# Two-bank AV tiles, half a mask on ScalarE, a new order of the first loads, and an earlier load for batch 1, in a pooled-attention and MLP kernel

## The chip, the cores and the metric

The kernel runs on one core of one Trainium2 chip. The time is device microseconds (us) of one execution; of the 60 runs of the kernel before that stand beside v_noact, 57 lie within 0.3% of their median of 300.84. Engines: PE (TensorE), PEld (its weight loads), DVE (VectorE), ACT (ScalarE), POOL (GpSimd) and SP (SyncE, which here only issues loads, stores and transposes by DMA). Every run comes with a state, fast or slow; a run is called slow when it is over 1.5% above the fastest of its kernel. Ratios in this text are the mean time of one kernel's fast runs over the mean time of the other's fast runs of the same rounds, so they are not quite the ratio of the medians that are quoted beside them. The span of a profile is some 1.7 us shorter than the time.

## The reference

```python
# q, k, v: (8 batches, 8 heads, 576 tokens, 64)
k_p = k.reshape(B, H, S // 8, 8, D).mean(axis=3)      # keys and values are pooled by 8: 72 of each
v_p = v.reshape(B, H, S // 8, 8, D).mean(axis=3)
scores = np.matmul(q, k_p.transpose(0, 1, 3, 2)) / np.sqrt(D)
attn = np.exp(scores - max) / sum                     # softmax
x = np.matmul(attn, v_p)                              # "AV"; then laid out as (4608 tokens, 512)
h = x @ w_in                                          # 512 -> 2048
return (h - np.tanh(h)) @ w_out                       # 2048 -> 512
```

The 72 pooled keys of a head are handled as 64 in four tiles (two heads to a tile) and the 8 that are left over, which are called the leftover keys.

## The kernel before

The MLP of one batch is one long run of matmuls on PE. Attention of the next batch is woven into it. Batch 0 has nothing to be woven into, so its attention, the *front*, is on the path; batch 1's loads are on their way meanwhile. Some words: an *hT* matmul belongs to x @ w_in and an *o_ps* matmul to the product with w_out; the AV matmuls write x; to *turn* x is to transpose it on PE, after which ACT copies (*evacuates*) it from PSUM; `warm_pe(n)` issues n filler matmuls whose result nobody uses; the *tail* of q is its last 64 tokens of a batch. The parts that matter:

```python
    # loads of batch 0: SP and ACT issue them in this order
    load_main(k_pairs, k_raw[0], 0, 0, 1); load_q0(0, 2)
    load_main(k_pairs, k_raw[0], 0, 1, 2); load_q0(2, 4)
    load_main(k_pairs, k_raw[0], 0, 2, 4)
    load_q0(4, 8)                                     # second half of q, from ACT
    load_dense(k_pairs, k_raw[0], 0, nc.scalar)       # leftover keys
    load_dense(v_pairs, v_raw[1], 0, nc.scalar)
    ...
    after(load_k(1), w1_dmas[1])                      # k of batch 1 once w1's second chunk is in
    load_q(1, False)                                  # q of batch 1 without its tail, from SP
    load_main(v_pairs, v_raw[1], 1, 0, NM)
    ...
    nc.scalar.dma_start(out=t0[:QT, :, R, :], ...)    # tail of q, batch 0, from ACT
    ...
    v_main(VB[0], vs, nc.vector, 0, 2)                # mask of v, two instructions on DVE
    v_main(VB[0], vs, nc.vector, 2, 4)
    load_left(v_pairs, v_raw[1], 1, nc.scalar)        # four small loads of batch 1, issued by ACT
    load_q_tail(1, q_raws[1], nc.scalar)              # tail of q of batch 1, issued by ACT
    ...
    av_half(0, 0, 0, xs[0], ps_all)                   # AV: eight half blocks, a PSUM bank each
    av_half(0, 1, 0, xs[1], ps_all)
    av_half(0, 2, 0, xs[2], ps_all)
    x_pe_transpose(0, 0, xs[0], (0, 2))               # transposed on PE, evacuated by ACT into xT
    ...
```

An engine issues its loads in the order of its own instruction stream.

The softmax here doesn't subtract the row's maximum and nothing guards it: scores larger than these inputs give would overflow.

Of the kernel before, what the change touches and what calls it, by code (L numbers as in the profile page):

```python
# [8 lines left out]
FP32 = mybir.dt.float32  # L9
BF16 = mybir.dt.bfloat16  # L10
ACT = mybir.ActivationFunctionType
ALU = mybir.AluOpType
# [25 lines left out]
def kernel(  # L38
# [19 lines left out]
    ps_h = ctx.enter_context(tc.tile_pool(name="ps_h", bufs=3, space=PSUM))  # L58
    ps_o = ctx.enter_context(tc.tile_pool(name="ps_o", bufs=2, space=PSUM))
    ps_a = ctx.enter_context(tc.tile_pool(name="ps_a", bufs=3, space=PSUM))  # L60
# [19 lines left out]
    q_bf = const.tile([128, R + 1, H, D], BF16, name="q_bf")  # L80
    warm = const.tile([128, 1], FP32, name="warm")
# [156 lines left out]

    def v_left(vb, vs, eng):
        eng.tensor_tensor(  # L240
            out=vb[:, 2 * NM :, 0:D],
            in0=vs.to_broadcast([128, NM, D]),
            in1=mask[:, 2 * NM :, :].to_broadcast([128, NM, D]),
            op=ALU.mult,
        )
# [92 lines left out]
    def av_half(b, blk, half, x_sb, alloc):  # L338
        E = E_tiles[b]
        vb = VB[b % 2]  # L340
        c0 = blk * 128 if blk < 4 else S - 128
        ps = alloc([128, 4, D1], FP32, "x_ps")
        for n in range(3):
# [14 lines left out]
        rden = work.tile([128, 4, 1], FP32, name="rden", tag="rden", bufs=4)  # L358
        nc.vector.reciprocal(out=rden[:, :, :], in_=ps[:, :, D:D1])  # L359
        nc.vector.tensor_tensor(  # L360
            out=x_sb[:, half, :, :],
            in0=ps[:, :, 0:D],
            in1=rden[:, :, :].to_broadcast([128, 4, D]),
            op=ALU.mult,
        )
# [56 lines left out]
    def mlp_h_mms(g, i, f0, f1, pool=None):  # L422
        tok0 = g * TG
        if f0 == 0:
            p, tag = pool or (ps_h, "hT_ps")
            h_tiles[i] = p.tile([128, TG], FP32, name="hT_ps", tag=tag)
# [96 lines left out]
    warm_ps = ps_o.tile([128, 512], FP32, name="warm_ps", tag="o_ps")  # L523
# [21 lines left out]
    load_q0(2, 4)  # L545
    load_main(k_pairs, k_raw[0], 0, 2, 4)
    load_q0(4, 8)
    load_dense(k_pairs, k_raw[0], 0, nc.scalar)
    load_dense(v_pairs, v_raw[1], 0, nc.scalar)
# [3 lines left out]
    nc.scalar.activation(out=warm[:, :], in_=warm[:, :], func=ACT.Exp)  # L553
    nc.vector.memset(KB[0][:, :], 0.0)
# [37 lines left out]
    after(load_k(1), w1_dmas[1])  # L592
# [49 lines left out]
    q_turn(nc.scalar.copy, 6, 8)  # L642
    pool_k(0, nc.vector, 2, 4)
    warm_pe(6)
    k_turn(2, 4)
    pool_k(0, nc.vector, NM, NT)
    warm_pe(2)
    q_pe_transpose(0, (2, 3), "act")
    warm_pe(2)
    scores_wide(0, (2, 3))  # L650
    k_turn_left()
    warm_pe(2)
    v_ps = v_pe_pool(NM, NT, spread)
    scores_wide(0, (NM,))
    v_left(VB[0], v_ps[:, 0, :, :], nc.vector)
    vs = v_pe_pool(0, NM, ident)
    v_main(VB[0], vs, nc.vector, 0, 2)
    v_main(VB[0], vs, nc.vector, 2, 4)
    load_left(v_pairs, v_raw[1], 1, nc.scalar)
    load_q_tail(1, q_raws[1], nc.scalar)  # L660
    xs = [new_x() for _ in range(4)]
    gts = []
    ps_o2 = lambda sh, dt, name: ps_o.tile(sh, dt, name=name, tag="o_ps")
    ps_h2 = lambda sh, dt, name: ps_h.tile(sh, dt, name=name, tag="hT_ps")
    warm_pe(2)
    av_half(0, 0, 0, xs[0], ps_all)
    av_half(0, 1, 0, xs[1], ps_all)
    av_half(0, 2, 0, xs[2], ps_all)
    x_pe_transpose(0, 0, xs[0], (0, 2))
    av_half(0, 3, 0, xs[3], ps_all)  # L670
    warm_pe(1)
    x_pe_transpose(0, 1, xs[1], (0, 2))
    ps_any = ps_b1
    av_half(0, 0, 1, xs[0], ps_h2)
    warm_pe(1)
    x_pe_transpose(0, 2, xs[2], (0, 2))
    av_half(0, 1, 1, xs[1], ps_b1)
    warm_pe(1)
    x_pe_transpose(0, 3, xs[3], (0, 2))
    av_half(0, 2, 1, xs[2], ps_o2)  # L680
    mlp_h_mms(0, 0, 0, 2)
    x_pe_transpose(0, 0, xs[0], (2, 4))
    av_half(0, 3, 1, xs[3], ps_b1)
    mlp_h_mms(0, 1, 0, 2)
    x_pe_transpose(0, 1, xs[1], (2, 4))
    mlp_h_mms(0, 2, 0, 2)
    x_pe_transpose(0, 2, xs[2], (2, 4))
# [117 lines left out]
```

## Time and profile before

| kernel before | |
|---|---|
| time, median of 3 runs | 301.34 us (301.06 to 301.42) |
| span of the profile | 299.1 us |
| PE busy | 291.5 us (97%) |
| first AV matmul of batch 0 | 14.61 us |
| PE without a break from | 20.41 us |
| waits of PE after that | near 32.5 and 37 us, 0.5 and 0.7 us (from matmul start to matmul start) |

The lines behind this are in the prediction below. In an order of time stand start, length, engine, line, operation; ACTq is ACT's sequencer, which issues the loads.

```profile
16.28 0.62 ACTq L127 DMA_DIRECT2D q_raw<-in_q_dram  x1
16.95 0.92 ACT L397 CAST xT<-xT_ps 128x256 bf16<-128x256 f32 x3 [3.19 <-PE x_ps L346]
```

L127 is the issue of the q tail of batch 1. It happens at 16.28 us because the q tail of batch 0 landed at 16.26, and the two share a semaphore (the trace, which keeps the semaphore of each issue, has both on number 100). The evacuations of the transposed x stand behind it. The second is DVE's pooling of v of batch 1:

```profile
42.32 0.82 DVE L219 TENSOR_TENSOR v_raw<-v_raw 128x640 f32<-128x640 f32 x1
...
44.31 0.42 DVE L240 TENSOR_TENSOR VB<-v_raw,mask 128x256 bf16<-128x256 f32 x1
```

### The profile page before, as it was taken

Reading aid. Unit: us, or ns where it says so; the run is one execution under the profiler, and the core shown is the slowest. Engines: PE = TensorE matmul, PEld = TensorE weight load, DVE = VectorE, ACT = ScalarE, POOL = GpSimd, SP = SyncE. Lnnn points to the kernel's source line nnn. Section 1 sums busy time; section 2 is a strip of 40 time slices with the busy share of each in tenths; the row PEclk is TensorE's granted clock in tenths of the full one; section 3 lists DMA queues with packets and bytes.
Section 4 is the critical chain, followed back from the end, with each engine's and each line's share of the span. In section 5 each row is a group of like instructions: output and inputs, shape, how many; then the busy total and the mean of one; then the engine's idle time right before and its main releaser. Section 6 shows DMA issues by size and latency. Waiting matters only on the chain.

```text
span 299.1 us, 4694 instructions
## 1 busy us (share of the span) xinstructions
PE 291.5 (97%) x1671; PEld 142.5 (48%) x1671; DVE 159.1 (53%) x343; ACT 149.4 (50%) x283; POOL 115.5 (39%) x110
## 2 busy tenths in 40 slices
PE   7989999999999999999999999999999999999994
PEld 3454455544544454445444554455445544444443
DVE  5658665673547444753476247716680758108600
ACT  4647583666146633654265516650665166126511
POOL 8500904871496109922971089307940000000000
PEclk9999999999999999999999999999999999999999
DMA  7999999849854998699648974897431430111032
GB/s 251 226 211 278 311 227 310 263 87 328 234 113 99 271 297 134 117 302 245 107 88 235 300 167 94 242 294 159 97 66 35 95 92 0 37 70 36 0 72 70
DMA packets 66183, 49.79 MB, mean 166 GB/s; under 512 B 39920, under 2 KB 52976, under 8 KB 66160
## 3 DMA queue, kind: packets, MB, share of 16 engines
q1 hardware_dynamic: 58832, 42.94, 56.0%
q0 software_dynamic: 4752, 4.72, 9.4%
q10 hardware_dynamic: 2576, 1.84, 2.3%
q8 instruction: 13, 0.21, 0.3%
q14 instruction: 10, 0.08, 0.1%
HBM read 36.70 MB, written 9.44 MB: 154 GB/s over the span
## 4 chain that ended last, share of the span: by engine, by line
PE 85%; DMA 9%; POOL 4%; issue 0%; SPq 0%; ACT 0%; DVE 0%; POOLq 0%
PE o_ps L456 40%; PE hT_ps L428 37%; DMA w1b<-in_moe_w_in_dram 4%; PE x_ps L346 4%; DMA k_raw<-in_k_dram 4%; PE s_ps L298 3%; POOL k_raw L198 1%; DMA out_dram<-o_sb 1%; POOL k_raw L203 1%; POOL kd L206 1%; POOL w2b L510 0%; PE xT_ps L390 0%; POOL v_raw L576 0%; PE qT_ps L171 0%; POOL w1b L503 0%
## 5 line engine op out<-in xcount | busy, mean ns | idle before, releaser
L456 PE MATMUL o_ps<-w2b,gT 128*128 128x512 bf16 x560 | 134.4, 380 | 0.0
L441 DVE TENSOR_TENSOR gT<-hT_ps,t_sb 128x512 bf16<-128x512 f32 x144 | 98.9, 691 | 57.7 <-ACT t_sb L439 57.6
L428 PE MATMUL hT_ps<-xT,w1b 128*128 128x512 bf16 x576 | 126.9, 379 | 0.3 <-ACT xT L397 0.3
L439 ACT ACTIVATE t_sb<-hT_ps 128x512 f32<-128x512 f32 x144 | 85.6, 597 | 38.3 <-PE hT_ps L428 37.5
L428 PEld LDWEIGHTS <-w1b 128*128 128x128 bf16 x576 | 55.9, 98 | 66.5 <-issue 0.4
L456 PEld LDWEIGHTS <-gT 128*128 128x128 bf16 x560 | 52.5, 98 | 52.0 <-issue 1.4
L465 ACT COPY o_sb<-o_ps 128x512 f32<-128x512 f32 x33 | 19.3, 585 | 75.2 <-PE o_ps L456 75.2
L359 DVE RECIPROCAL rden<-x_ps 128x4 f32<-128x4 f32 x80 | 14.2, 177 | 52.5 <-PE x_ps L346 52.0
L360 DVE TENSOR_TENSOR x_sb<-x_ps,rden 128x256 bf16<-128x256 f32 x80 | 34.0, 425 | 3.5 <-DMA xT<-x_sb 0.6
L148 POOL CAST q_bf<-q_raw 128x2048 bf16<-128x2048 f32 x6 | 11.3, 1888 | 59.9 <-issue 34.8
L198 POOL TENSOR_TENSOR k_raw<-k_raw 128x1280 f32<-128x1280 f32 x7 | 20.2, 2886 | 27.4 <-DMA k_raw<-in_k_dram 16.6
L317 ACT ACTIVATE E<-s_ps 128x288 bf16<-128x288 f32 x60 | 21.4, 410 | 13.2 <-PE s_ps L298 13.0
L346 PE MATMUL x_ps<-VB,E 128*128 128x130 bf16 x240 | 20.8, 221 | 0.4 <-ACT xT L397 0.3
L346 PEld LDWEIGHTS <-E 128*128 128x128 bf16 x240 | 16.9, 98 | 8.8 <-DVE VB L230 0.6
L216 POOL TENSOR_TENSOR v_raw<-v_raw 128x1280 f32<-128x1280 f32 x6 | 17.4, 2898 | 0.0
L298 PE MATMUL s_ps<-qT,KB 128*128 128x288 bf16 (+5 forms) x128 | 17.0, 290 | 0.2
L298 PEld LDWEIGHTS <-KB 128*128 128x128 bf16 (+1 forms) x128 | 7.0, 96 | 10.2 <-issue 3.5
L527 PE MATMUL warm_ps<-xT 128*128 128x512 bf16 x29 | 10.2, 465 | 1.3 <-DVE xT L539 1.3
L206 POOL TENSOR_TENSOR kd<-k_raw 128x640 bf16<-128x640 f32 x7 | 10.8, 1540 | 0.5
L203 POOL TENSOR_TENSOR k_raw<-k_raw 128x640 f32<-128x640 f32 x7 | 10.8, 1541 | 0.5
L397 ACT CAST xT<-xT_ps 128x256 bf16<-128x256 f32 (+1 forms) x14 | 5.8, 436 | 8.5 <-PE xT_ps L390 5.1
L219 POOL TENSOR_TENSOR v_raw<-v_raw 128x640 f32<-128x640 f32 x6 | 9.3, 1544 | 0.5
(73 smaller groups left out, 100.7 us busy)
## 6 DMA issues: line engine op xcount, KB each, us to landing
k_raw<-in_k_dram SPq DMA_DIRECT2D x7, 1024.0 KB, 5.9
q_raw<-in_q_dram SPq DMA_DIRECT2D x7, 1024.0 KB, 10.2
v_raw<-in_v_dram SPq DMA_DIRECT2D x7, 1024.0 KB, 9.3
out_dram<-o_sb SPq DMA_DIRECT2D x38, 128.0 KB, 2.4
out_dram<-o_sb SPq DMA_DIRECT2D x16, 256.0 KB, 3.7
w1b<-in_moe_w_in_dram POOLq DMA_DIRECT2D x4, 512.0 KB, 14.2
w2b<-in_moe_w_out_dram POOLq DMA_DIRECT2D x4, 512.0 KB, 16.9
k_raw<-in_k_dram SPq DMA_DIRECT2D x7, 128.0 KB, 5.8
```

The lines of the kernel that those rows point to most:

```text
L198: first = eng.tensor_tensor(out=r[:, :, 0:4, :], in0=r[:, :, 0:4, :], in1=r[:, :, 4:8, :], op=ALU.add)
L216: eng.tensor_tensor(out=r[:, :, 0:4, :], in0=r[:, :, 0:4, :], in1=r[:, :, 4:8, :], op=ALU.add)
L298: nc.tensor.matmul(dst[p : p + w], lhsT=KB[b % 2][:, o : o + w], rhs=qTs[b][:, m, c0:c1], start=True, stop=True,)
L317: nc.scalar.activation(out=E[:, t, half * hs : (half + 1) * hs], in_=ps[:, :], func=ACT.Exp, scale=SCALE)
L346: nc.tensor.matmul(ps[:, 2 * n : 2 * n + 2, :].rearrange("p h d -> p (h d)") if n < 2 else ps.rearrange("p (a s) d -> p a s d", s=2)[:, :, ...
L359: nc.vector.reciprocal(out=rden[:, :, :], in_=ps[:, :, D:D1])
L360: nc.vector.tensor_tensor(out=x_sb[:, half, :, :], in0=ps[:, :, 0:D], in1=rden[:, :, :].to_broadcast([128, 4, D]), op=ALU.mult,)
L428: nc.tensor.matmul(h_tiles[i][:, :], lhsT=w1b[:, fb, i * 128 : (i + 1) * 128], rhs=xT[:, fb, tok0 : tok0 + TG], start=(fb == 0), stop=(fb ...
L439: nc.scalar.activation(out=t_sb[:, :], in_=h_ps[:, :], func=ACT.Tanh)
L441: nc.vector.tensor_sub(out=gT[:, :], in0=h_ps[:, :], in1=t_sb[:, :])
L456: nc.tensor.matmul(o_ps[:, :], lhsT=gts[i][:, tb * 128 : (tb + 1) * 128], rhs=w2b[:, i, :], start=(i == 0), stop=(i == NHID - 1),)
L465: (nc.vector.tensor_copy if g == 0 and tb % 2 else nc.scalar.copy)(out=o_sb[:, :], in_=o_ps[:, :])
```

## The change

The intent is a shorter front and a filled hole at 37 us. (1) AV of batch 0 works on two blocks at once in tiles of two PSUM banks: four reciprocals and four multiplies on DVE in place of eight each, and larger evacuations of the transposed x. Half of v's mask goes to ACT. (2) The leftover keys are loaded and scored ahead of the second half of k, and the second half of q is issued later. (3) k of batch 1 is released by w1's first chunk. (4) One PSUM tile whose banks are dealt out by hand, which (1) needs. Cut to its core:

```diff
-    ps_h = ctx.enter_context(tc.tile_pool(name="ps_h", bufs=3, space=PSUM))   # and ps_o, ps_a
+    PS = psum.tile([128, 8, 512], FP32, name="PS")
+    ps_h, ps_o, ps_a = Banks(0, 1, 2), Banks(3, 4), Banks(5, 6, 7)            # (shortened)
...
+    def v_main_act(vb, vs, t0, t1):
+        for h in range(2):
+            nc.scalar.activation(
+                out=vb[:, 2 * t0 + h : 2 * t1 : 2, 0:D], in_=vs[:, t0:t1, 0, :],
+                func=ACT.Copy, scale=mask[:, h, :],
+            )
...
+    load_dense(k_pairs, k_raw[0], 0)
     load_main(k_pairs, k_raw[0], 0, 2, 4)
-    load_q0(4, 8)
-    load_dense(k_pairs, k_raw[0], 0, nc.scalar)
-    load_dense(v_pairs, v_raw[1], 0, nc.scalar)
+    load_dense(v_pairs, v_raw[1], 0)
     nc.scalar.activation(out=warm[:, :], in_=warm[:, :], func=ACT.Exp)
+    load_q0(4, 8)
...
-    after(load_k(1), w1_dmas[1])
+    after(load_k(1), w1_dmas[0])
...
+    pool_k(0, nc.vector, NM, NT)
     pool_k(0, nc.vector, 2, 4)
...
-    scores_wide(0, (2, 3))
-    k_turn_left()
+    scores_wide(0, (2, 3, NM))
...
     v_main(VB[0], vs, nc.vector, 0, 2)
-    v_main(VB[0], vs, nc.vector, 2, 4)
+    v_main_act(VB[0], vs, 2, 4)
     load_left(v_pairs, v_raw[1], 1, nc.scalar)
     load_q_tail(1, q_raws[1], nc.scalar)
...
-    av_half(0, 0, 0, xs[0], ps_all)          # eight of these, with their transposes
+    av_pair(0, 0, 0)                         # four of these
+    av_pair(1, 0, 2)
+    av_pair(0, 1, 5)
+    x0_turn((0, 1), 0, 7, nc.scalar.copy)
+    av_pair(1, 1, 0)
+    x0_turn((2, 3), 0, 2, nc.scalar.copy)
+    x0_turn((0, 1), 1, 7, nc.scalar.copy)
...
```

More of the change, by code (lines that the diff above doesn't have):

```diff
@@ L57, with bank, __init__, tile @@
     opool = ctx.enter_context(tc.tile_pool(name="opool", bufs=4))
-    ps_h = ctx.enter_context(tc.tile_pool(name="ps_h", bufs=3, space=PSUM))
-    ps_o = ctx.enter_context(tc.tile_pool(name="ps_o", bufs=2, space=PSUM))
-    ps_a = ctx.enter_context(tc.tile_pool(name="ps_a", bufs=3, space=PSUM))
+    psum = ctx.enter_context(tc.tile_pool(name="psum", bufs=1, space=PSUM))
+    PS = psum.tile([128, 8, 512], FP32, name="PS")
+    def bank(i, shape):
+        n = 1
+        for d in shape[1:]:
+            n *= d
+        v = PS[:, i, 0:n]
+        if len(shape) == 3:
+            return v.rearrange("p (a b) -> p a b", a=shape[1])
+        if len(shape) == 4:
+            return v.rearrange("p (a b c) -> p a b c", a=shape[1], b=shape[2])
+        return v
+    class Banks:
+        def __init__(self, *ids):
+            self.ids, self.n = ids, 0
+        def tile(self, shape, dtype=None, name=None, tag=None):
+            self.n += 1
+            return bank(self.ids[(self.n - 1) % len(self.ids)], shape)
+    ps_h = Banks(0, 1, 2)
+    ps_o = Banks(3, 4)
+    ps_a = Banks(5, 6, 7)
     ctx.enter_context(tc.manual_schedule())
@@ L80 @@
     q_bf = const.tile([128, R + 1, H, D], BF16, name="q_bf")
+    x0 = const.tile([128, 4, 2, 4, D], BF16, name="x0")
     warm = const.tile([128, 1], FP32, name="warm")
@@ L237, in v_main @@
         )
+    def v_main_act(vb, vs, t0, t1):
+        for h in range(2):
+            nc.scalar.activation(
+                out=vb[:, 2 * t0 + h : 2 * t1 : 2, 0:D],
+                in_=vs[:, t0:t1, 0, :],
+                func=ACT.Copy,
+                scale=mask[:, h, :],
+            )
     def v_left(vb, vs, eng):
@@ L338, in av_half, with av_mms @@
     def av_half(b, blk, half, x_sb, alloc):
+        ps = alloc([128, 4, D1], FP32, "x_ps")
+        av_mms(b, blk, half, ps)
+        rden = work.tile([128, 4, 1], FP32, name="rden", tag="rden", bufs=4)
+        nc.vector.reciprocal(out=rden[:, :, :], in_=ps[:, :, D:D1])
+        nc.vector.tensor_tensor(
+            out=x_sb[:, half, :, :],
+            in0=ps[:, :, 0:D],
+            in1=rden[:, :, :].to_broadcast([128, 4, D]),
+            op=ALU.mult,
+        )
+    def av_mms(b, blk, half, ps):
         E = E_tiles[b]
@@ L341, in av_half @@
         c0 = blk * 128 if blk < 4 else S - 128
-        ps = alloc([128, 4, D1], FP32, "x_ps")
         for n in range(3):
@@ L357, in av_half @@
             )
-        rden = work.tile([128, 4, 1], FP32, name="rden", tag="rden", bufs=4)
-        nc.vector.reciprocal(out=rden[:, :, :], in_=ps[:, :, D:D1])
-        nc.vector.tensor_tensor(
-            out=x_sb[:, half, :, :],
-            in0=ps[:, :, 0:D],
-            in1=rden[:, :, :].to_broadcast([128, 4, D]),
-            op=ALU.mult,
-        )
     def new_x():
@@ L424, in mlp_h_mms @@
         if f0 == 0:
-            p, tag = pool or (ps_h, "hT_ps")
-            h_tiles[i] = p.tile([128, TG], FP32, name="hT_ps", tag=tag)
+            h_tiles[i] = ps_h.tile([128, TG]) if pool is None else pool
         for fb in range(f0, f1):
@@ L521, in after @@
             )
-    warm_ps = ps_o.tile([128, 512], FP32, name="warm_ps", tag="o_ps")
+    warm_ps = bank(4, [128, 512])
     def warm_pe(n, cols=512):
@@ L642 @@
     q_turn(nc.scalar.copy, 6, 8)
+    pool_k(0, nc.vector, NM, NT)
     pool_k(0, nc.vector, 2, 4)
-    warm_pe(6)
+    warm_pe(3)
+    k_turn_left()
+    warm_pe(5)
     k_turn(2, 4)
-    pool_k(0, nc.vector, NM, NT)
-    warm_pe(2)
     q_pe_transpose(0, (2, 3), "act")
     warm_pe(2)
-    scores_wide(0, (2, 3))
-    k_turn_left()
+    scores_wide(0, (2, 3, NM))
+    v_ps = v_pe_pool(NM, NT, spread)
+    v_left(VB[0], v_ps[:, 0, :, :], nc.vector)
     warm_pe(2)
-    v_ps = v_pe_pool(NM, NT, spread)
@@ L654 @@
-    scores_wide(0, (NM,))
-    v_left(VB[0], v_ps[:, 0, :, :], nc.vector)
     vs = v_pe_pool(0, NM, ident)
     v_main(VB[0], vs, nc.vector, 0, 2)
-    v_main(VB[0], vs, nc.vector, 2, 4)
+    v_main_act(VB[0], vs, 2, 4)
     load_left(v_pairs, v_raw[1], 1, nc.scalar)
     load_q_tail(1, q_raws[1], nc.scalar)
-    xs = [new_x() for _ in range(4)]
     gts = []
-    ps_o2 = lambda sh, dt, name: ps_o.tile(sh, dt, name=name, tag="o_ps")
-    ps_h2 = lambda sh, dt, name: ps_h.tile(sh, dt, name=name, tag="hT_ps")
@@ L665 @@
-    warm_pe(2)
-    av_half(0, 0, 0, xs[0], ps_all)
-    av_half(0, 1, 0, xs[1], ps_all)
-    av_half(0, 2, 0, xs[2], ps_all)
-    x_pe_transpose(0, 0, xs[0], (0, 2))
-    av_half(0, 3, 0, xs[3], ps_all)
-    warm_pe(1)
-    x_pe_transpose(0, 1, xs[1], (0, 2))
-    ps_any = ps_b1
-    av_half(0, 0, 1, xs[0], ps_h2)
-    warm_pe(1)
-    x_pe_transpose(0, 2, xs[2], (0, 2))
-    av_half(0, 1, 1, xs[1], ps_b1)
-    warm_pe(1)
-    x_pe_transpose(0, 3, xs[3], (0, 2))
-    av_half(0, 2, 1, xs[2], ps_o2)
@@ L681, with av_pair @@
-    mlp_h_mms(0, 0, 0, 2)
-    x_pe_transpose(0, 0, xs[0], (2, 4))
-    av_half(0, 3, 1, xs[3], ps_b1)
-    mlp_h_mms(0, 1, 0, 2)
-    x_pe_transpose(0, 1, xs[1], (2, 4))
-    mlp_h_mms(0, 2, 0, 2)
-    x_pe_transpose(0, 2, xs[2], (2, 4))
-    x_pe_transpose(0, 3, xs[3], (2, 4))
-    mlp_h_mms(0, 3, 0, 2, (ps_o, "o_ps"))
-    mlp_h_mms(0, 4, 0, 2, (ps_o, "o_ps"))
+    def av_pair(p, half, b0):
+        ps = PS[:, b0 : b0 + 2, 0 : 4 * D1].rearrange("p k (h d) -> p k h d", d=D1)
+        for k in range(2):
+            av_mms(0, 2 * p + k, half, ps[:, k, :, :])
+        rden = work.tile([128, 2, 4, 1], FP32, name="rden2", tag="rden2")
+        nc.vector.reciprocal(out=rden[:, :, :, :], in_=ps[:, :, :, D:D1])
+        nc.vector.tensor_tensor(
+            out=x0[:, 2 * p : 2 * p + 2, half, :, :],
+            in0=ps[:, :, :, 0:D],
+            in1=rden[:, :, :, :].to_broadcast([128, 2, 4, D]),
+            op=ALU.mult,
+        )
@@ new lines, in x0_turn @@
+    def x0_turn(blks, half, b0, eng):
+        n = len(blks)
+        ps = bank(b0, [128, 2, n, 128])
+        for i, blk in enumerate(blks):
+            for f in range(2):
+                nc.tensor.matmul(
+                    ps[:, f, i, :],
+                    lhsT=x0[:, blk, half, 2 * f : 2 * f + 2, :].rearrange("p h d -> p (h d)"),
+                    rhs=ident[:, :],
+                    start=True,
+                    stop=True,
+                )
+        c = blks[0] * 128
+        eng(
+            out=xT[:, 2 * half : 2 * half + 2, c : c + n * 128],
+            in_=ps.rearrange("p f i c -> p f (i c)"),
+        )
@@ new lines, in h_open @@
+    def h_open(i, b0):
+        mlp_h_mms(0, i, 0, 2, bank(b0, [128, TG]))
+    warm_pe(2)
+    av_pair(0, 0, 0)
+    av_pair(1, 0, 2)
+    av_pair(0, 1, 5)
+    warm_pe(2)
+    x0_turn((0, 1), 0, 7, nc.scalar.copy)
+    av_pair(1, 1, 0)
+    warm_pe(2)
+    x0_turn((2, 3), 0, 2, nc.scalar.copy)
+    warm_pe(2)
+    x0_turn((0, 1), 1, 7, nc.scalar.copy)
+    h_open(3, 3)
+    h_open(4, 4)
+    x0_turn((2,), 1, 5, nc.scalar.copy)
+    x0_turn((3,), 1, 6, nc.vector.tensor_copy)
+    h_open(2, 2)
@@ L691 @@
+    h_open(0, 0)
+    h_open(1, 1)
+    ps_any = ps_b1
+    ps_h.n = ps_o.n = 0
     nc.scalar.copy(out=q_bf[:QT, R, :, :], in_=t0[:QT, :, R, :])
```

## The prediction

> **What bounds the kernel now.** I read the page's busy table first, then busy time by stage, then each engine's order of time in the first 40 us, and last the chain that ended last. From the page, and from the view by stretches (start:end, length, then busy us of PE, PEld, DVE, ACT, POOL, granted clock, DMA share, GB/s):
>
> ```profile
> PE 291.5 (97%) x1671; PEld 142.5 (48%) x1671; DVE 159.1 (53%) x343; ACT 149.4 (50%) x283; POOL 115.5 (39%) x110
> ...
> 14.60:20.40 5.80, 4.82 (x49) 3.16 (x50) 4.59 (x17) 2.04 (x6) 0.00 (x0) 1.00 1.24 215
> 20.40:32.00 11.60, 11.60 (x72) 5.60 (x68) 8.43 (x15) 8.78 (x17) 1.79 (x1) 1.00 1.16 259
> 32.00:36.90 4.90, 4.58 (x25) 2.05 (x24) 3.24 (x7) 2.54 (x6) 4.81 (x5) 1.00 1.11 332
> 36.90:40.00 3.10, 2.58 (x22) 1.43 (x21) 0.98 (x3) 2.82 (x5) 0.86 (x1) 1.00 1.19 260
> ```
>
> PE is the bound: from 20.4 us on it is full except for two holes near 32.5 and 37 us. The chain's long pieces are 64 hT matmuls in 13.81 us, so 0.216 us each[...]; nothing after 40 us can give anything, because the change leaves the later PE work alone. So the change can gain only (a) in how soon PE gets into its uninterrupted stream of MLP matmuls, and (b) in those holes. The order of time on PE shows both (start, length, count, idle before and who ended it):
>
> ```profile
> 14.61 0.69 PE L346 MATMUL x_ps<-VB,E 128*128 128x130 bf16 x9
> ...
> 18.49 0.59 PE L428 MATMUL hT_ps<-xT,w1b 128*128 128x512 bf16 x2 [0.28 <-ACT xT L397]
> ...
> 20.41 5.78 PE L428 MATMUL hT_ps<-xT,w1b 128*128 128x512 bf16 x26
> ...
> 32.75 0.23 PE L390 MATMUL xT_ps<-ident,x_sb 128*128 128x64 bf16 x2 [0.32 <-DVE x_sb L360]
> ...
> 37.82 0.45 PE L259 MATMUL kT_ps<-ident,kd 128*128 128x128 bf16 x5 [0.52 <-POOL kd L206]
> ```
>
> AV of batch 0 starts at A = 14.61. Six hT matmuls are done before 20.41; from there PE isn't interrupted, so the tenth is issued out at 20.41 + 4 x 0.216 = 21.27, that is A + 6.66. Ten is the count to compare: after ten (five tiles, first half) the changed kernel also runs free. What sets 6.66 is DVE, which takes a half block every 0.55 us, eight times:
>
> ```profile
> 15.00 0.18 DVE L359 RECIPROCAL rden<-x_ps 128x4 f32<-128x4 f32 x1
> 15.22 0.42 DVE L360 TENSOR_TENSOR x_sb<-x_ps,rden 128x256 bf16<-128x256 f32 x1
> 15.56 0.17 DVE L359 RECIPROCAL rden<-x_ps 128x4 f32<-128x4 f32 x1
> ...
> 19.63 0.43 DVE L360 TENSOR_TENSOR x_sb<-x_ps,rden 128x256 bf16<-128x256 f32 x1
> ```
>
> What fixes A is the chain before it: q heads 4 to 7 land at 8.96 (issued 1.84; ACT's cast starts when they do), casts, transposes, scores, then v's pooling on PE (1.05 us) and v's mask on DVE. And the hole at 37 us is the end of a chain of loads (start, length, what):
>
> ```profile
> 8.98 1.14 ACT L610 CAST q_bf<-q_raw 128x512 bf16<-128x512 f32 x2 [0.18 <-DMA q_raw<-in_q_dram]
> ```
> ```profile
> 5.86 12.86 DMA w1b<-in_moe_w_in_dram
> 19.21 10.84 DMA k_raw<-in_k_dram
> 30.21 2.90 POOL k_raw L198
> ...
> 36.23 1.55 POOL kd L206
> ```
>
> Batch 1's k isn't issued until the second chunk of w1 has landed (18.72), lands by 30.05, is pooled on GpSimd until 37.77, and PE waits for it. Counted from matmul start to matmul start the hole is 0.68 us (four o_ps matmuls begin at 36.28, so PE could take the next at 37.14).
>
> [...] 128x256 takes 0.425 us and 128x512 (gT) 0.692, so 1.04 ns an element and 0.158 us fixed. [...] ACT's and DVE's halves of v's mask read one bank. [...] from 5 to 7 us SP's ring (2048-byte packets) moved 0.50 MB and ACT's (1024-byte) 0.26 MB.
>
> **The change part by part.**
>
> 1. *Pairs in AV.* DVE: a pair needs one reciprocal (about 0.18) and one 128x512 multiply, 0.692. Spacing is now 0.548 = 0.217 (reciprocal to multiply) + 0.424 - 0.09 overlap; for a pair 0.217 + 0.692 - 0.09 = 0.82. Four pairs 3.3 us in place of eight halves 4.4. Evacuations of the transposed x fall from eight of 128x256 (0.37 each) to three of 128x512 (0.585) plus one small each on ACT and DVE. The PE work (24 AV matmuls at 0.059, 16 transposes at 0.056) is the same. Walking through from A: first pair's six matmuls end at A+0.51; DVE has x of it at A+0.55+0.91 = A+1.46, the others at 2.28, 3.09, 3.91. PE: three pairs to 1.05, two fillers, transposes of blocks 0-1 at 1.52, fourth pair to 2.09, fillers to 2.52, transposes of 2-3 to 2.74 (end 2.91). ACT evacuates the first by 2.53 and the second from 2.94 to 3.54. Third transposes at 3.18 (x at 3.09). Tile 3's hT opens at 3.59, when ACT is done; tile 4 at 4.02; last four transposes 4.45 to 4.67; the other three tiles to 5.97. The second halves then need x evacuated by 5.3: no wait. So A + 5.97 in place of A + 6.66: 0.69 gained.
>
> 2. *Leftover keys first, q later.* The leftover k goes to SP's queue ahead of the second k half, and heads 4 to 7 of q are issued after the table load, near 3.3 in place of 1.84. DVE's 1.1 us of leftover pooling moves into its wait before 7.86, and the leftover scores follow the others directly. Against it: 0.25 MB (leftover k and v) now stands ahead of q's second half[...]. At 0.34 MB/us (2 MB land between about 2.5 and 8.96) with half the rate after 8 us I put q's landing at 9.6 to 10.4, middle 9.9, in place of 8.96. Then: casts to 11.07, transposes of the last heads to 11.3, ACT's qT to 12.14, scores 11.76 to 12.64, leftover v to 12.88, two fillers (0.43, new there) to 13.31, v's pooling to 14.18 (end 14.35), DVE's mask 0.43 and A = 14.87. ACT's half of the mask[...] comes after DVE's on the same bank[...] and is first needed by the third pair at 15.6: just hidden. So part 2 costs 0.26 where the serial order had hoped to gain; if q lands at 9.0 it gains 0.15.
>
> 3. *Batch 1 sooner.* k waits for w1's first chunk (15.43) rather than its second: 3.3 us sooner. GpSimd then ends near 34.5 and PE's need is near 36.7, so the whole 0.68 us goes. The price is traffic: k competes with w1's third and fourth chunks (22.06 and 26.46 now). I put the fourth at 28.4 (0.09 to 0.12 MB/us of written bytes beside k, as w1 and w2 had beside k from 23 to 33 us), needed at 30.0; w2's first at 32.7, needed at 34.1. No wait.
>
> 4. *One PSUM tile with banks by hand.* 98 waits of PE on itself vanish. They cost nothing: matmuls with such a wait follow their predecessor at the usual 0.058 us.
>
> Sum: 0.69 - 0.26 + 0.68 = 1.1 us; 301.34 - 1.1 = 300.2.
>
> **The rivals.** *q's second half rules the front*: the loads are the critical resource in the first 12 us (DMA share 1.1 to 1.2 there). If it lands at 10.5 or later, A goes to 15.5, parts 1 and 2 cancel and only part 3 is left: 300.7. *w1's second chunk becomes the wait*: it landed at 18.71, and tile 4's hT wants it at 14.87 + 4.02 = 18.89. Batch 1's k, issued at 15.4, can push it out if its packets start at once; before, k's packets began 3.8 us after issue, which speaks against. At 20 us it would cost 1.1: 301.3. *The hole at 37 us only moves*: the saved 0.4 us makes PE come earlier, and the w2 chunks or q's cast (which now waits for its load until 36.6) could stop it; the wait list shows 1.3 us for that cast, but it has nearly 2 us of slack before PE needs it. Then 300.6. *The front gains fully*: q at 9.0, A = 14.45, and 299.8.
>
> **Range and chances.** Both gains that I trust, 0.69 and 0.68, are small shares of 301, and the disputed term moves by about 0.6 either way. So 300.2, with 299.5 to 300.9 for eight in ten. A change over 2% would need 6 us: between 12 and 40 us PE loses only some 3.5 us to spacings over the usual and 1.5 us to seven fillers of 0.216, 5 us together (so one in a hundred for faster), and a slow-down of 6 us would need a load order gone badly wrong.
>
> **What would show it.** Right: pair multiplies of about 0.69 us spaced 0.82; first AV matmul between 14.4 and 15.4; first hT matmul 3.6 us after it, tenth done 6.0 after it; q heads 4-7 landing after 9.5 with ACT waiting for them; no PE wait for kd near 37 us; k of batch 1 issued near 15.5. Wrong: PE waiting for w1 before tile 4 or 8, a mask by ACT that holds up the third pair, or new PE gaps after 40 us, which would mean that the bank tracking orders engines in the steady state.

## The result, and the profile after

The changed kernel takes 317.19 us, median of four runs (311.50 to 319.82), beside 301.38 for the kernel before on the same chip. Two of the four runs count as slow (319.2 and 319.8); over the fast ones the ratio is 1.040, 95% interval 1.029 to 1.050. By the fast runs the change makes the kernel slower by some 4%. The recorded profile is of a slow run. The same kernel run again gave 314.22 (313.11 to 318.41), ratio 1.043, with a profile; where its numbers differ they are given too.

The page (busy us, share of the span, instructions; then tenths of PE's busy time and of its granted clock in 40 slices of 8 us):

```profile
PE 295.4 (93%) x1643; PEld 145.4 (46%) x1674; DVE 166.0 (52%) x335; ACT 149.2 (47%) x281; POOL 117.7 (37%) x110
...
PE   8743999499999999999999999999999999999995
...
PEclk9995899869999999999999999999999999999999
```

PE is emptier in slices 3 and 4 and has another gap in slice 8. In each, and after it, its granted clock is down: the trace has it at 0.50 from 24.25 to 34.49 us and from 61.80 to 68.62, and at 1.00 from 7.18 us to the first of these and between them. In the kernel before it is 1.00 from 6.54 us to the end. By stages (columns as in the prediction):

```profile
20.40:32.00 11.60, 3.09 (x13) 1.69 (x14) 0.42 (x1) 2.37 (x5) 3.81 (x3) 0.67 1.15 270
32.00:36.90 4.90, 4.90 (x18) 1.96 (x17) 1.48 (x3) 2.29 (x6) 3.65 (x3) 0.75 1.16 275
36.90:40.00 3.10, 3.10 (x19) 1.45 (x17) 3.06 (x6) 2.29 (x4) 0.00 (x0) 1.00 1.13 287
```

Between 20.4 and 32 us, where PE had been full, it is busy for 3.1 of 11.6 us. No wait is left near 37 us, but PE is ten microseconds late there, so this run can't tell whether the hole was filled as predicted; b_dep0 below can. PE's order of time:

```profile
16.32 1.23 PE L389 MATMUL PS<-VB,E 128*128 128x130 bf16 x18 [0.16 <-DVE VB L253]
...
28.68 0.59 PE L714 MATMUL PS<-ident,x 128*128 128x128 bf16 x4 [8.93 <-ACT xT L722]
29.17 0.58 PE L462 MATMUL PS<-xT,w1b 128*128 128x512 bf16 x1
```

AV begins at 16.32 us, not 14.61. Four matmuls that turn x wait 8.93 us for ACT's evacuation of an earlier tile. The hT matmul after the wait takes 0.58 us where 0.38 is usual, and the next ones start 0.43 us apart and not 0.216, twice the spacing at a granted clock of 0.50. The next view is of ACT:

```profile
16.88 1.38 ACTq L129 DMA_DIRECT2D v_raw<-in_v_dram  x3
27.38 0.63 ACTq L150 DMA_DIRECT2D q_raw<-in_q_dram  x1
28.05 1.07 ACT L722 CAST xT<-PS 128x512 bf16<-128x512 f32 x2 [11.06 <-DMA k_raw<-in_k_dram]
```

ACT did nothing. From 18.26 to 27.38 us it stands in one issue, the q tail of batch 1 (L150), and the evacuations (L722) are behind it. The release named at the end is the landing of k of batch 1. The chain of waits has the same:

```profile
16.35 11.01 DMA k_raw<-in_k_dram
...
27.38 0.63 ACTq L150
...
28.05 0.59 ACT xT L722
```

k of batch 1 lands at 27.36 us and ACT goes on 0.02 us later. In this trace the two loads report on the same semaphore, number 102. In the kernel before, k was on 102 too, but the q tail was on 100, with a load that had landed already. The second gap, from the list of waits (engine, line, waited for, total us, times, longest):

```profile
PE PS L389 <- DVE VB L272: 3.3, 1, 3.3
```

This is AV of batch 1 at 63.56 us, waiting for v of batch 1, which DVE pools:

```profile
53.83 2.04 DVE L242 TENSOR_TENSOR v_raw<-v_raw 128x640 f32<-128x640 f32 x1
...
59.84 3.67 DVE L272 TENSOR_TENSOR VB<-v_raw,mask 128x256 bf16<-128x256 f32 x1
```

The same two instructions took 0.82 and 0.42 us before. There they ended before GpSimd began; here they run beside it:

```profile
52.52 2.67 POOL L226 TENSOR_TENSOR k_raw<-k_raw 128x640 f32<-128x640 f32 x1
55.27 2.00 POOL L229 TENSOR_TENSOR kd<-k_raw 128x640 bf16<-128x640 f32 x1
```

GpSimd's own took less before:

```profile
51.53 1.53 POOL L203 TENSOR_TENSOR k_raw<-k_raw 128x640 f32<-128x640 f32 x1
53.15 1.54 POOL L206 TENSOR_TENSOR kd<-k_raw 128x640 bf16<-128x640 f32 x1
```

In the profile of the fast state (after_again) PE's first wait is 8.7 us and the second 1.7 us.

The AV pairs themselves did what the prediction said: multiplies of 0.69 us, 0.83 us apart.

```profile
17.18 0.69 DVE L702 TENSOR_TENSOR x<-PS,rden 128x512 bf16<-128x512 f32 x1
...
18.01 0.69 DVE L702 TENSOR_TENSOR x<-PS,rden 128x512 bf16<-128x512 f32 x1
```

### The profile page after: what moved, and what is told of

It reads as the page before. It is cut to its first block, busy times and chain, and to the rows that moved or that the text cites.

```text
span 318.1 us, 4683 instructions
## 1 busy us (share of the span) xinstructions
PE 295.4 (93%) x1643; PEld 145.4 (46%) x1674; DVE 166.0 (52%) x335; ACT 149.2 (47%) x281; POOL 117.7 (37%) x110
## 4 chain that ended last, share of the span: by engine, by line
PE 82%; DMA 10%; DVE 4%; POOL 1%; issue 1%; SPq 1%; ACT 0%; ACTq 0%; POOLq 0%
PE PS L462 39%; PE PS L490 36%; PE PS L389 4%; DMA w1b<-in_moe_w_in_dram 4%; DMA k_raw<-in_k_dram 3%; PE PS L330 3%; DMA v_raw<-in_v_dram 2%; DVE VB L272 1%; DMA out_dram<-o_sb 1%; DVE v_raw L239 1%; DVE VB L253 1%; DVE v_raw L242 1%; DVE v_raw L245 1%; PE PS L425 0%; PE PS L714 0%
## 5 line engine op out<-in xcount | busy, mean ns | idle before, releaser
L490 PE MATMUL PS<-w2b,gT 128*128 128x512 bf16 x542 | 133.8, 383 | 1.2 <-issue 0.3
L475 DVE TENSOR_TENSOR gT<-PS,t_sb 128x512 bf16<-128x512 f32 x144 | 98.9, 691 | 59.4 <-ACT t_sb L473 59.1
L462 PE MATMUL PS<-xT,w1b 128*128 128x512 bf16 x564 | 128.1, 384 | 0.9 <-issue 0.4
L473 ACT ACTIVATE t_sb<-PS 128x512 f32<-128x512 f32 x144 | 85.6, 597 | 40.6 <-PE PS L462 39.9
L499 ACT COPY o_sb<-PS 128x512 f32<-128x512 f32 x33 | 19.3, 585 | 75.2 <-PE PS L490 72.3
L374 DVE RECIPROCAL rden<-PS 128x4 f32<-128x4 f32 x72 | 12.7, 176 | 52.5 <-PE PS L389 52.2
L375 DVE TENSOR_TENSOR x_sb<-PS,rden 128x256 bf16<-128x256 f32 x72 | 30.5, 424 | 2.5
L221 POOL TENSOR_TENSOR k_raw<-k_raw 128x1280 f32<-128x1280 f32 x7 | 20.2, 2885 | 28.4 <-DMA k_raw<-in_k_dram 28.4
L349 ACT ACTIVATE E<-PS 128x288 bf16<-128x288 f32 x60 | 21.4, 410 | 13.2 <-PE PS L330 13.0
L389 PE MATMUL PS<-VB,E 128*128 128x130 bf16 x240 | 20.9, 224 | 4.2 <-DVE VB L272 3.3
L239 POOL TENSOR_TENSOR v_raw<-v_raw 128x1280 f32<-128x1280 f32 x6 | 17.4, 2900 | 0.0
L330 PE MATMUL PS<-qT,KB 128*128 128x288 bf16 (+5 forms) x128 | 16.8, 289 | 0.1
L330 PEld LDWEIGHTS <-KB 128*128 128x128 bf16 (+1 forms) x128 | 7.0, 96 | 10.9 <-issue 3.9
## 6 DMA issues: line engine op xcount, KB each, us to landing
q_raw<-in_q_dram SPq DMA_DIRECT2D x7, 1024.0 KB, 10.4
```

The costliest lines, as they stand in the source:

```text
L221: first = eng.tensor_tensor(out=r[:, :, 0:4, :], in0=r[:, :, 0:4, :], in1=r[:, :, 4:8, :], op=ALU.add)
L239: eng.tensor_tensor(out=r[:, :, 0:4, :], in0=r[:, :, 0:4, :], in1=r[:, :, 4:8, :], op=ALU.add)
L330: nc.tensor.matmul(dst[p : p + w], lhsT=KB[b % 2][:, o : o + w], rhs=qTs[b][:, m, c0:c1], start=True, stop=True,)
L349: nc.scalar.activation(out=E[:, t, half * hs : (half + 1) * hs], in_=ps[:, :], func=ACT.Exp, scale=SCALE)
L374: nc.vector.reciprocal(out=rden[:, :, :], in_=ps[:, :, D:D1])
L375: nc.vector.tensor_tensor(out=x_sb[:, half, :, :], in0=ps[:, :, 0:D], in1=rden[:, :, :].to_broadcast([128, 4, D]), op=ALU.mult,)
```

## The experiments

The theory: the change moved the q tail of batch 1 onto the semaphore of k of batch 1, by nothing more than the order in which the build deals them out, and ACT is held until k lands. Rivals: (R1) the sooner k, by its traffic; (R2) the later second half of q; (R3) the two-bank tiles. All outputs are right.

### First: is it the issue?

**v_early.** ACT's five issues ahead of the masks:

```diff
+    load_left(v_pairs, v_raw[1], 1, nc.scalar)
+    load_q_tail(1, q_raws[1], nc.scalar)
     v_main(VB[0], vs, nc.vector, 0, 2)
     v_main_act(VB[0], vs, 2, 4)
-    load_left(v_pairs, v_raw[1], 1, nc.scalar)
-    load_q_tail(1, q_raws[1], nc.scalar)
```

> The changed kernel with ScalarE's five load issues (the leftovers of v and the tail of q, both of batch 1) moved ahead of the masking of v in program order; every load, matmul and evacuation is otherwise the same. In the build the tail of q then waits for a load that landed long before, no longer for k of batch 1. Theory (ScalarE sits in the issue of the q tail until k of batch 1 lands): the 8.9 us idle time of TensorE near 20 us is gone, the granted clock does not fall, the late stall near 60 us goes too, and what is left is the later front, the shorter AV part and the missing hole at 37 us: 301.3 + 1.7 - 0.7 - 0.7 = 301.6, 300.5 to 302.5. Rival 1 (the sooner k load itself and its traffic): still 311 to 317. Rival 2 (the later half of q) and rival 3 (the two-bank AV tiles): still above 308, since all of that is still there.

**v_dep1.** The changed kernel without the sooner k:

```diff
-    after(load_k(1), w1_dmas[0])
+    after(load_k(1), w1_dmas[1])
```

> The changed kernel with k of batch 1 released by the second chunk of w1 again, as before the change; the rest is as changed, and in the build the tail of q still waits for k of batch 1. Theory: k of batch 1 lands at about 30 us in place of 27.4, ScalarE is held until then, so the idle time of TensorE grows from 8.9 to 11 or 12 us and the time gets no better: 313 to 321 us, slower than the changed kernel by 1 to 3 us in runs of one state. Rival 1 (the sooner load of k is what hurts): 301 to 302 us, with the idle time gone.

**b_act.** The kernel before, with only the second mask on ACT:

```diff
-    v_main(VB[0], vs, nc.vector, 2, 4)
+    v_main_act(VB[0], vs, 2, 4)
```

> The kernel before with only this taken from the change: the second half of the mask of v goes to ScalarE in two instructions instead of to VectorE. AV in single banks, the load order and the release of k are as before. In the build, the tail of q then waits for k of batch 1 (in the kernel before: for the tail of q of batch 0). Theory: ScalarE is held from about 17 us to 29.4 us, when k of batch 1 lands, the x evacuations and the tanh behind it wait, TensorE idles 9 to 12 us: 311 to 320 us. Rivals 1, 2 and 3 (sooner k, later q, two-bank tiles): none of them is in this kernel, so 300.8 to 301.8 us.

**b_dep0.** The kernel before, with only the sooner k:

```diff
-    after(load_k(1), w1_dmas[1])
+    after(load_k(1), w1_dmas[0])
```

> The kernel before with only k of batch 1 released by the first chunk of w1 instead of the second. The tail of q still waits for a load that has long landed. Theory: the hole of 0.68 us at 37 us goes and nothing else moves: 300.7 us, 300.2 to 301.2. Rival 1 (the sooner k load takes bandwidth from the weights or stalls an engine): 305 us or more. If k sooner delays the second chunk of w1 by the size of its transfer (some 3 us) past its first use, there is a new hole near 33 to 38 us and the time is 301 to 303 us.

| run | median us | range | ratio to before (301.06) | 95% interval |
|---|---|---|---|---|
| v_early | 302.08 | 301.99 to 302.14 | 1.0031 | 1.0015 to 1.0046 |
| v_dep1 | 320.22 | 318.26 to 321.08 | 1.0624 | 1.0594 to 1.0655 |
| b_act | 317.69 | 316.51 to 320.71 | 1.0564 | 1.0524 to 1.0605 |
| b_dep0 | 300.24 | 300.08 to 302.53 | 0.9983 | 0.9960 to 1.0007 |

The theory foretold which two of the four would be slow, and R1 to R3 fall. Moving five issues ahead of the masks takes 11 to 12 us away (ratios of fast runs, against 1.040 and 1.043), with all parts of the change in place. Undoing the sooner k doesn't help but leaves the hold longer, since k lands later (PE waits 10.0 us in place of 8.9; 11 or 12 were expected):

```profile
28.70 0.62 ACTq L150 DMA_DIRECT2D q_raw<-in_q_dram  x1
29.36 1.07 ACT L722 CAST xT<-PS 128x512 bf16<-128x512 f32 x2 [12.14 <-DMA k_raw<-in_k_dram]
```

And b_act makes the whole loss out of the kernel before by two instructions that have nothing to do with loads; ACT is held there from 16.9 to 28.4 us:

```profile
28.39 0.62 ACTq L127 DMA_DIRECT2D q_raw<-in_q_dram  x1
29.05 0.92 ACT L406 CAST xT<-xT_ps 128x256 bf16<-128x256 f32 x3 [13.42 <-DMA k_raw<-in_k_dram]
```

In every trace that has the hold the evacuation behind the issue has the landing of k as what ended the idle time before it: 11.06 us of it in after, 10.77 in after_again, 12.14 in v_dep1, 13.42 in b_act, 10.62 in v_fill, 10.82 in v_pool_after. In four traces without the hold ACT's issue of the tail goes out at 16.28 us (the kernel before), 16.07 (v_an_dep1), 16.45 (v_noact) and 16.61 (v_early). How much longer v_dep1 and b_act take than the changed kernel should not be read from their medians: a run's state is told from the fastest of its own kernel, and all their runs, though listed as fast, have a mean clock of 0.967 to 0.978, as the slow runs of the changed kernel do (0.972 to 0.977; its fast ones 0.976 to 0.987). b_dep0's gain, 0.5 us by the means, isn't clear of noise here; it was run again below.

v_early still shows a small copy of the fault. ACT's order of time there:

```profile
16.61 0.64 ACTq L150 DMA_DIRECT2D q_raw<-in_q_dram  x1
17.29 0.63 ACT L264 ACTIVATE VB<-PS,mask 128x128 bf16<-128x128 f32 x2 [2.68 <-DVE rden L701]
```

The issue waits, as in the kernel before, for the q tail of batch 0 (landed 16.59); the masks are now behind it, and PE waits 1.1 us for them.

### Second: what are the parts worth without the hold?

**v_noact** puts the mask back on DVE in the changed kernel:

```diff
-    v_main_act(VB[0], vs, 2, 4)
+    v_main(VB[0], vs, nc.vector, 2, 4)
```

> The changed kernel with the mask of v of batch 0 wholly on VectorE again, as before the change; nothing else is touched. In the build the tail of q then waits for a load that landed at about 16.5 us. Theory: no idle time of 9 us, and the 1.1 us that TensorE waited in v_early for ScalarE's mask (which stood behind the issue of the q tail there) is gone too: 302.1 - 1.1 + 0.1 = 301.1 us, 300.6 to 301.8. Rival (the mask on ScalarE is only one of several things that hold ScalarE): above 308 us. Rival (the 1.1 us lie beside other work): as v_early, 302.1.

**v_an_front** is v_noact with the order of loads and of leftover keys as before:

```diff
-    load_dense(k_pairs, k_raw[0], 0)
     load_main(k_pairs, k_raw[0], 0, 2, 4)
-    load_dense(v_pairs, v_raw[1], 0)
+    load_q0(4, 8)
+    load_dense(k_pairs, k_raw[0], 0, nc.scalar)
+    load_dense(v_pairs, v_raw[1], 0, nc.scalar)
...
-    load_q0(4, 8)                                  # after the table load
... (pool_k, k_turn, k_turn_left, scores_wide in the order of before)
```

> Of the change only the two-bank AV pairs (with the one bank-managed PSUM tile) and the sooner k of batch 1 are left; the mask of v is on VectorE, the order of the first loads and of the leftover keys is as before the change. If parts 1 and 3 are worth what was worked out in the prediction (0.69 and 0.68 us), 301.1 - 1.4 = 299.7 us, 299.2 to 300.3, under both kernels. If the pairs gain nothing since TensorE's part between them takes their place, 300.3, as with the sooner k alone.

**v_an_dep1** is v_an_front without the sooner k, so the AV pairs alone:

```diff
-    after(load_k(1), w1_dmas[0])
+    after(load_k(1), w1_dmas[1])
```

> As v_an_front, with k of batch 1 released by the second chunk of w1 again: the AV pairs alone. If they are worth 0.69 us: 300.4 us, 300.0 to 300.8. If they are worth nothing: 301.1. If the bank-managed tile costs time by its 98 fewer self-waits or by coarser tracking: above 301.4.

**b_loads** is the kernel before with part 2 alone (the reverse of v_an_front's diff).

> The kernel before with only the order of the first loads and of the leftover keys from the change (the second half of q issued later, the leftover keys ahead of the second half of k); k of batch 1, AV and the mask as before. The prediction put this at +0.26 us: 301.3. The traces of after and v_early say that the second half of q lands at 10.7 us in place of 9.0 and that the last keys come later by about as much, so +1.4 to +1.7: 302.2 to 302.9 us.

| run | parts in it | median us | runs | ratio to before (300.84) | 95% interval |
|---|---|---|---|---|---|
| v_noact | 1 (no ACT mask), 2, 3, 4 | 301.60 | 17 | 1.0034 | 1.0021 to 1.0046 |
| v_an_front | 1 (no ACT mask), 3, 4 | 300.14 | 22 | 0.9981 | 0.9971 to 0.9991 |
| v_an_dep1 | 1 (no ACT mask), 4 | 300.94 | 22 | 1.0009 | 0.9999 to 1.0020 |
| b_loads | 2 | 302.11 | 12 | 1.0041 | 1.0022 to 1.0059 |

v_noact is 0.5 us over the middle of what was expected, within its range. For b_loads, 302.2 to 302.9 was expected from the traces of after and v_early; it came to 302.1, a loss of 1.2 us by the mean of the runs, just under that range and far from the 0.26 of the prediction. v_an_front is the one kernel of this set that beats both, by 0.19%. The surprise is v_an_dep1: 300.4 was expected, 300.9 came, so the pairs alone show no gain (the interval excludes the 0.69), and with the sooner k (v_an_front against b_dep0: 0.9981 against 0.9983) nothing that the interval can show either.

### Third: what the hold costs beyond its length

**after_again**, the changed kernel unedited, as a yardstick.

> The changed kernel once more, unedited, as the yardstick for the two runs beside it on the same chip: 311 to 320 us, mostly 315 to 319, TensorE's mean granted clock 0.97 to 0.98.

**v_fill** keeps PE busy while ACT is held:

```diff
-    warm_pe(2)
+    warm_pe(42)
     x0_turn((0, 1), 1, 7, nc.scalar.copy)
```

> The changed kernel with 40 more warm-up matmuls on TensorE (about 8.6 us) ahead of the transposes that wait for ScalarE, so that TensorE is busy while ScalarE is held; ScalarE is held as before until k of batch 1 lands. If the fall of the granted clock after the idle time is a cost of its own, the clock between 20 and 37 us is 1.00 in place of 0.67 to 0.75 and the first pass of batch 0 ends some 2.4 us sooner. What of it reaches the end: 2 to 3 us (below after_again by that) if the late stall near 60 us stays as it is; next to nothing if VectorE, which is slowed by GpSimd there, sets that stall and only makes it longer by what was gained. Rival (the lower clock is a property of these runs and not of the idle time): the clock stays under 0.8 there, and the time is that of after_again.

**v_pool_after** keeps GpSimd off while DVE pools v of batch 1:

```diff
-            pool_v(1, nc.vector)
+            v1_done = pool_v(1, nc.vector)           # returns its last instruction
...
-    pool_k(2, nc.gpsimd)
+    after([pool_k(2, nc.gpsimd)], v1_done)
```

> The changed kernel with GpSimd's pooling of k of batch 2 held until VectorE's pooling of v of batch 1 is done; ScalarE is held as before. Theory (the two engines, which overlap only because VectorE is late, slow each other): VectorE's five operations fall back from about 2.3, 2.0, 1.7, 2.3 and 3.7 us to 1.5, 0.8, 0.5, 0.7 and 0.4 us, the waits of 0.8 and 3.3 us near 60 us go, and with them the second fall of the clock (some 1.7 us): 4 to 6 us below after_again. Rival (the operations are slower for another reason, or k of batch 2 comes too late now): the durations stay, or a new wait near 75 us takes the gain.

**best2** tries for more from v_an_front:

```diff
     h_open(3, 3)
-    h_open(4, 4)
...
     h_open(1, 1)
+    h_open(4, 4)
```

> v_an_front with the fifth hT tile opened last of the five, not second. In v_an_front TensorE waited 0.3 us at 18.3 us for the second chunk of w1 (landed 18.8), which this tile needs and the first four do not. If this wait cost the end its 0.3 us: 299.8 us against 300.14 of v_an_front. If the later weights (second chunk of w2, landed at 38.4 there just as it was needed) set the end of this stage: 300.1, no gain.

| run | median us | range | ratio to before (300.96) | 95% interval |
|---|---|---|---|---|
| after_again | 314.22 | 313.11 to 318.41 | 1.0432 | 1.0411 to 1.0454 |
| v_fill | 313.36 | 311.76 to 316.07 | 1.0446 | 1.0398 to 1.0493 |
| v_pool_after | 312.13 | 311.17 to 312.79 | 1.0373 | 1.0351 to 1.0394 |
| best2 | 300.67 | 299.74 to 302.47 | 0.9991 | 0.9973 to 1.0009 |

In v_fill's profile the clock between 20.4 and 32 us is 1.00, beside 0.57 there in after_again's:

```profile
20.40:32.00 11.60, 11.44 (x59) 5.42 (x59) 0.73 (x2) 2.53 (x5) 3.69 (x3) 1.00 1.15 270
```

PE is busy there for 11.44 of 11.60 us, beside 3.34 in after_again. So in this pair of traces the clock falls with the idle time and stays up without it. What the fall costs at the end stays open: the fast runs of the two can't be told apart (1.0446 and 1.0432), and v_fill's range is 4 us wide.

In v_pool_after DVE's operations have their old length again, all five of them (two are shown):

```profile
51.57 0.83 DVE L242 TENSOR_TENSOR v_raw<-v_raw 128x640 f32<-128x640 f32 x1
...
53.56 0.42 DVE L272 TENSOR_TENSOR VB<-v_raw,mask 128x256 bf16<-128x256 f32 x1
```

PE waits for none of them. That the two engines slowed each other is thus shown: DVE's two operations take 0.83 and 0.42 us here and took 2.04 and 3.67 in the changed kernel, and GpSimd's two take 1.53 and 1.54 us here and took 2.67 and 2.00. By what mechanism they do so was not shown. In the trace of the changed kernel DVE's second addition began at 53.83, GpSimd's ended at 55.19, and DVE's ended at 55.87, which is 0.68 us later and near the 0.83 that it takes alone. The gain was 1.8 us (313.85 to 312.06, means of the fast runs), not the 4 to 6 that I expected. That figure was read from the profile of a slow run, where PE's wait was 3.3 us; in the fast state it is 1.7 us.

best2 showed no gain; its own profile is of a run whose first loads happened to land late, so it doesn't tell whether the wait for w1 was removed for nothing or was not removed.

### Fourth: why the AV pairs are worth nothing

**b_fill3** and **b_dep0_fill3** make PE's front 0.65 us longer in the kernel before and in b_dep0; **b_dep0_again** is the yardstick:

```diff
-    warm_pe(2)
+    warm_pe(5)
     av_half(0, 0, 0, xs[0], ps_all)
```

> The kernel before with three more warm-up matmuls (3 x 0.216 = 0.65 us of TensorE) ahead of the first AV matmul: the front of the kernel before made 0.65 us longer. If the wait for k of batch 1 at 37 us (0.68 us there) takes up what the front loses or gains, the time is that of the kernel before, +0.0 to +0.15 us, and that wait is near 0 in the trace; then a gain of 0.69 us in front of it is lost in the same way. If the front reaches the end: +0.65 us.

> b_dep0 (sooner k, no hole at 37 us) with the same three matmuls. If the front now sets the end: +0.65 us against b_dep0_again. If weights that arrive just in time take up the difference: +0.0 to +0.3 us, and the trace of b_dep0_again then shows waits for w1 or w2 that shrink here.

> b_dep0 unedited, as the yardstick for b_dep0_fill3 on the same chip: 300.1 to 300.4 us, the kernel before minus 0.6 to 0.8.

**v_tail_spq** moves the one issue to SP, and leaves the rest of the change:

```diff
     load_q(1, False)
+    load_q_tail(1, q_raws[1], nc.sync)
...
-    load_q_tail(1, q_raws[1], nc.scalar)
```

> The changed kernel with the one issue of the q tail of batch 1 moved from ScalarE to SyncE, behind the main part of q; ScalarE's mask, the load order, the AV pairs and the sooner k stay. Theory: ScalarE is never held, so no idle time of 9 us and full clock: 301.3 to 302.2 us as in v_noact, perhaps 0.1 less by the mask on ScalarE. Rival (something else of the change holds ScalarE or TensorE too): above 304 us.

| run | median us | runs | ratio to before (300.72) | 95% interval |
|---|---|---|---|---|
| b_fill3 | 301.03 | 14 | 1.0007 | 0.9994 to 1.0020 |
| b_dep0_fill3 | 300.37 | 14 | 0.9989 | 0.9974 to 1.0003 |
| b_dep0_again | 300.37 | 22 | 0.9988 | 0.9978 to 0.9999 |
| v_tail_spq | 302.99 | 4 | 1.0071 | 1.0050 to 1.0092 |

Three more matmuls in the front of PE cost 0.1 to 0.2 us by the means, not 0.65 (which lies just outside b_fill3's interval), with the hole at 37 us and without it. So the hole is not what takes the difference up, and for b_fill3 my expectation named the wrong place: its trace still has a wait of 0.74 us there (k landed at 30.2 us in that run). The traces say where it goes. In the kernel before, PE stood 0.25 us ahead of the first AV matmul, for v's mask, and the third turn of x, at 16.86 us, was followed by 0.46 us in which PE waited for ACT. Both are absent from the traces of b_fill3 and b_dep0_fill3. (b_fill3's first loads landed late in that run besides, so b_dep0_fill3 is the better witness: AV starts 0.72 us later than in the kernel before, at 15.33, and the tenth hT matmul is issued out only 0.37 us later, at 21.64.) The second of them is again ACT in the issue of the q tail, until the tail of batch 0 lands, at 15.9 to 16.3 us in these three traces, though PE comes to AV up to 1.0 us later in two of them.

That shows what the pairs can give. Counting from the first AV matmul to the tenth hT matmul issued out, as the prediction does, the kernel before had 6.66 us in its profile. In five traces of unpaired AV where the front came later, ACT was free by then, and it was 6.25 (b_dep0, b_dep0_again) and 6.31 (b_fill3, b_dep0_fill3, b_loads). With pairs it is 6.07, in v_an_dep1 (14.51 to 20.58) as in v_noact (16.52 to 22.59). The pairs save 0.2 us; 0.4 of the 0.69 belonged to that wait for ACT. And where they do bring PE forward, it waits longer for k of batch 1, which comes when its load lets it. In v_an_dep1:

```profile
37.41 0.45 PE L291 MATMUL PS<-ident,kd 128*128 128x128 bf16 x5 [0.80 <-POOL kd L229]
```

0.80 us, against 0.52 in the kernel before. With the sooner k that wait is gone, but in v_an_front PE came 0.3 us too soon for w1's second chunk, and at 85.37 us it lost 0.6 us to a DMA that writes a later xT from x.

A sum over the traces bears this out. In the eleven traces with neither the hold nor many missing records, the time from the tenth hT matmul to the end of the span, less PE's waits in it (from start to start), is 276.6 to 276.8 us. So what the front gains does reach the end, except for the waits that follow. In its one profile v_an_dep1 was 0.70 us ahead at the tenth matmul, waited 0.28 us more for k, and ended 0.3 us ahead; but one profile of the front says little. In the seven traces that have the old order of loads and no added fillers, AV starts anywhere from 14.39 to 17.45 us, as the first loads land, and b_dep0 itself was profiled at 300.69 us (AV at 15.62) and at 302.10 (17.05). The kernel before, with AV at 14.61, was caught at the early end, where the wait for ACT is in the sum.

v_tail_spq is free of the hold, so the place of this one issue is the cause; but it is 1 us slower than expected. Its trace has a new wait, for v of batch 1, whose load now lands at 45.0 us (42.1 in v_early), behind the tail on the same queue:

```profile
48.76 0.72 PE L389 MATMUL PS<-VB,E 128*128 128x130 bf16 x6 [1.13 <-DVE VB L253]
```

## Why the prediction was wrong

It said 300.2 us, same within 2%; the kernel took 317 (313.3 by the mean of its fast runs).

**The step that failed is ACT's first evacuation of the turned x.** The prediction's walk from A has "ACT evacuates the first by 2.53"; in the changed kernel that evacuation began at 28.05 us, which is A + 11.73. What the walk lacks is the issue in front of it. It costs every operation and transfer that the change touches, but takes the issues on ACT for granted: "load_q_tail" is the same line in both kernels, and so it counted as unmoved. The change moved it onto the semaphore of k of batch 1, and of its parts the mask on ACT is what did so: b_act has that alone and is held, v_noact lacks that alone and is not. ACT was held for 9.1 us, PE idled 8.8 to 8.9 us, and the rest of the loss came in its wake. In the fast profile of after_again the parts add up as follows: idle 8.8 us, 1.6 us for six matmuls at the low clock (0.57 between 20.4 and 32 us; counted from start to start: five 0.21 us late each, the first 0.59), and 1.9 us for the wait for v of batch 1, in all 12.3. Its span is 312.0 us and that of v_noact 299.8, so 12.2. The wait belongs to the sum as an effect of lateness: GpSimd's work on batch 2 begins by its loads, at 49 us in either kernel, while PE and DVE are ten microseconds late and so meet it.

In the traces of both kernels no issue of SP or ACT that shares a semaphore goes out before the earlier load has landed (188 such issues in each): 16.28 after 16.26 in the kernel before, 27.38 after 27.36 in the changed one.

**Part 1, pairs, -0.69.** The duration and spacing of DVE's work were right (0.69 and 0.83 us), and A + 5.97 was nearly so (6.07). The sentence that failed is "What sets 6.66 is DVE". About 0.4 us of it was ACT held by the tail of batch 0, which the trace of the kernel before shows as a late first evacuation (16.95 us, right after the issue), and which the prediction didn't ask about. DVE itself, said to set the pace, stood idle 0.47 us before its eighth half block, waiting for PE (the row at 19.41 us of its order of time, which the prediction left out of its view). Measured alone, the part shows no gain (+0.1%, interval -0.0 to +0.2%).

**Part 2, load order, +0.26.** The direction was right, the size was not: +1.2 us alone (b_loads). The term mis-sized is the landing of q's second half: 10.4 to 10.9 us in all nine traces with this order, against 9.9 in the estimate (whose rate was high for its own figures: 2 MB in 6.46 us is 0.31 MB/us, not 0.34). That the rate halves after 8 us was the estimate; between 8.2 and 9.2 us the trace of the kernel before has 0.17 MB moved on ACT's queue and 0.09 on GpSimd's. With it the second half of k lands later too, at 9.4 to 10.0 in place of 7.8, and PE waits for its pooled form (2.2 us in b_loads), which the prediction left out. The rival that q rules the front named 10.5 us for the landing and was the better one for this part, though AV came later still than its 15.5 (16.0 to 17.4). The old order varies as well (q at 8.8 to 10.5 us, k at 7.5 to 9.5 in its nine traces), so the size rests on b_loads' runs and not on single traces.

**Part 2, ACT's mask.** That it would be just hidden was the estimate. Measured, the two instructions take 0.37 and 0.36 us; they read the bank that DVE's half reads, and the first began at 16.36, after DVE's, which the trace names as what ended its wait, had ended at 16.27. The cost of the mask was not in its length but in what it moved in the build.

**Part 3, sooner k, -0.68.** The hole at 37 us is gone in every trace that has it and not the hold, and k was issued at 16.35 us after w1's first chunk (landed 16.33), as the step says. Worth -0.4 to -0.5 us by the means of the two measurements; w1's fourth chunk landed at 29.5 us in b_dep0 (28.4 was estimated), and no wait of PE there is for a weight.

**Part 4** cost nothing that shows: v_an_dep1, which has it, is within 0.2% of the kernel before.

Without the hold the changed kernel is at 301.6 us (v_noact): still outside the range of 299.5 to 300.9, because part 2 costs what parts 1 and 3 were to bring.

The prediction gave no figure for a slow-down of over 2%; it said that this "would need a load order gone badly wrong", from adding up what was known to move. What went wrong was not the order or the traffic of loads but what one issue waits for. The trace of the kernel before had a warning in it: ACT's last issue goes out 0.02 us after a landing that it doesn't need.

## What to carry to other kernels

Here one issue of a load on a compute engine held that engine until another, unrelated load had landed: ACT for 9.1 us in the changed kernel, for 11.5 us in b_act. Before trusting an edit near such an issue, look in the instruction order of the build for what each issue waits for, and compare that before and after, also for issues that the edit leaves alone. Put such issues ahead of a stretch in which the engine isn't needed (v_early: 302.08 us, with 1.1 us of PE's time still lost to the masks behind the issue), or on a queue of an engine that computes nothing, and look at what then stands behind them there (v_tail_spq: 302.99 us, with v of batch 1 landing at 45.0 us, not 42.1). A part's gain that is read from one trace is worth only what remains when the waits inside it that end at a fixed time are taken out, and a front that starts with loads needs more than one trace.
